# The first batch's k and v cast on their way in, half tables mirrored, and the residual summed in PSUM

## The chip, the cores and the metric

The kernel runs on one core of a Trainium2 chip. The metric is the device time of one execution in microseconds (us), here as a median of three runs. The engines are called as in the profile: PE (TensorE matmul), PEld (its weight load), DVE (VectorE), ACT (ScalarE), POOL (GpSimd), SP (SyncE). DMAs are issued from SP (the hardware queue) and from POOL (the software queue).

## The reference

The computation has two stages. The first is a retention recurrence per batch and head, the second mixes the result by a Fourier transform over positions and channels, adds it to itself, normalizes, and runs two dense layers with a residual. There are 4 batches, 8 heads, 768 positions, a head width of 64, so a model width of 512 and a hidden width of 2048.

```python
gamma = 1.0 - 2.0 ** (-5.0 - np.arange(H))
for t in range(S):
    state = gamma * state + einsum('bhd,bhe->bhde', k[:, :, t], v[:, :, t])
    y[:, :, t] = scale * einsum('bhd,bhde->bhe', q[:, :, t], state)
x = y.transpose(0, 2, 1, 3).reshape(B, S, H * D)

mixed = np.real(np.fft.fft(np.fft.fft(x, axis=1), axis=2))
u = x + mixed
un = (u - mean(u)) / sqrt(var(u) + 1e-6)
out = u + relu(un @ w_ch1) @ w_ch2
```

## The kernel before

**Recurrence.** Positions are cut into 6 chunks of 128, heads are taken two at a time (four head pairs, in the order 0, 1, 3, 2; index `i` counts in that order). Per pair, q and k are turned by PE transposes (`tq`), their products (`wkA`) are masked by DVE into `atm` (L471 in the first batch, L603 later), chunk states (`wkK`) are run forward by a scan (L495) or by steps (L629), and the two parts of y are summed in PSUM (`wkY`) and evicted to `x` by ACT (L539, L662).

**Mixing.** The transform uses symmetry. `fold_s` builds sums and differences of the two halves of the positions (`xab`, L679), `fold_d` of the channels (`eo`, L689); `s1_unit` (L736) multiplies by the position tables `csp`, `ssp` to give `g`; `s2_unit` (L849, L853) multiplies `g` by the channel tables `cd16`, `sd16` and DVE puts both halves of `u` together from P and Q (L862, L864) with `qn`, an eviction of Q by ACT (L861). `g0_unit` makes the column that the folds leave out. For the first three of the six blocks of 128 rows of batch 0, x itself is put into the same PSUM tile by `px_unit` (L803) with halved identities. The tables are made in the kernel: `trig_dve` makes reduced angles on DVE (L288 to L292), `t_act` takes sines on ACT (L316 to L325).

**Dense layers.** `h0_unit` (L953) for the first half of batch 0, by blocks of 128 rows and groups of four of the 16 hidden blocks; `h_unit` (L936) elsewhere; `ch_unit` (L979, four parts per 128 rows) is the second layer. The weights come in eight pieces: four `w1_unit` (L993) and four `w2_unit` (L1000), casting DMAs issued from POOL.

**Order.** SP issues batch 0's loads first: q, k, v of each pair, f32, 384 KB each (L165). `first_units()` is a list written out by hand. Each unit's instructions are pinned behind the earlier ones on each engine (`pin`), so that every engine works its part of the list in that order. `filler(n)` puts n matmuls without use on PE. What follows the list is emitted by `emit`: the streams of `majors` (the dense layers) and of the next batch's attention are spread over a common axis and sorted; the place of a major in batch 0 is its number divided by their count. The second batch's loads (`load_unit(1, i, 6)`) wait for the seventh of the eight weight pieces, `w_dma[6]`, and for `lb[0]["mm"]`, the last matmul of the eighth `h0_unit`:

```python
if after is not None:
    for x in (w_dma[after].ins, lb[0]["mm"].ins):
        tc.add_manual_dep(dma.ins, x.name, ...)
```

In batch 0 POOL casts q (L398), scales and casts k (L407, L410) and casts v (L423) from f32 tiles; in batch 1 `cast_unit` does the same (L373, L383, L388).

Of the kernel before, what the change touches and what calls it, by code (L numbers as in the profile page):

```python
# [18 lines left out]
P = 128  # L19
# [10 lines left out]
PAIR_ORDER = [0, 1, 3, 2]  # L30
ON_ACT = {'q': (0, 1, 0), 'kv': (1, 1, 1), 'g': (0, 1, 1), 'gr': (0, 0, 0)}
# [12 lines left out]
def kernel(  # L44
# [13 lines left out]
    def pool(name, bufs, **kw):  # L58
# [3 lines left out]
    inp = pool("inp", 11)  # L62
# [33 lines left out]
        "p (n w) -> p n w", n=4)  # L96
    pmask = const.tile([P, 4], f32, tag="pmask")
# [60 lines left out]
    def load_unit(b, i, after=None):  # L158
        def run():
            h0 = 2 * PAIR_ORDER[i]  # L160
            for name, src in srcs.items():
                t = inp.tile([P, 2, NCH, D], f32, tag="in32", name=f"{name}32")
# [17 lines left out]
    for i in range(4):  # L180
        load_unit(0, i)()
# [3 lines left out]
    icol = const.tile([P, 8], f32, tag="icol")  # L185
    lgrow = const.tile([P, H], f32, tag="lgrow")
    gexp = const.tile([P, 2, H], f32, tag="gexp")
    gq8, gkd = gexp[:, 0], gexp[:, 1]
# [3 lines left out]
    kf_i = tmp[:, 0, 0:KN].bitcast(i32)  # L192
    kf = tmp[:, 1, 0:KN]
    rs = [tmp[:, 2 + n] if n < 4 else tmp2[:, n - 4] for n in range(10)]
# [6 lines left out]
    nc.gpsimd.iota(kf_i, pattern=[[1, KN]], base=0, channel_multiplier=0)  # L201
    nc.gpsimd.memset(wz, 0.0)  # L202
    filler(6)()
    for h in range(H):
        nc.vector.memset(lgrow[:, h:h + 1], float(lng[h]))
    nc.vector.memset(maskf, 1.0)
    nc.vector.tensor_copy(icol[:, 0:6], icol_i[:, 0:6])
    nc.vector.tensor_scalar(out=gexp[:, 0], in0=lgrow, scalar1=icol[:, 3:4],
                            scalar2=float(math.log(0.125)), op0=ALU.mult, op1=ALU.add)
    nc.vector.tensor_scalar(out=gexp[:, 1], in0=lgrow, scalar1=icol[:, 5:6], scalar2=None,  # L210
                            op0=ALU.mult)
    nc.scalar.activation(gexp, gexp, AF.Exp, bias=0.0, scale=1.0)
    for h2 in range(2):
        nc.scalar.activation(gk2[D * h2:D * h2 + D], lgrow[D * h2:D * h2 + D, h2:H:2], AF.Exp,
                             bias=0.0, scale=float(P))
    nc.scalar.activation(icol[:, 6:7], lgrow[:, 0:1], AF.Sin, bias=0.0, scale=1.0)
    make_identity(nc, ident16)
    nc.gpsimd.affine_select(out=maskf, in_=maskf, compare_op=ALU.is_ge, fill=0.0, base=0,
                            pattern=[[1, P]], channel_multiplier=-1)
    nc.gpsimd.memset(hpi, float(np.pi / 2))  # L220
    nc.gpsimd.memset(epsT, 1e-6)
    nc.gpsimd.memset(gk5[:, :, :, 0:1], 0.0)
    nc.vector.tensor_scalar(out=icoln[:, 0:3], in0=icol[:, 0:3],
                            scalar1=float(np.float32(1.0 / S)), scalar2=None, op0=ALU.mult)
    nc.vector.tensor_scalar(out=icoln[:, 3:5], in0=icol[:, 3:5], scalar1=float(1.0 / DM),
                            scalar2=None, op0=ALU.mult)
    nc.vector.tensor_copy(kf, kf_i)

    def gk_unit(hp):
        def run():  # L230
            nc.scalar.copy(gk5[:, hp, :, 1:], gk2[:, hp:hp + 1].unsqueeze(1).to_broadcast(
                [P, D, NCH - 2]))
        return run
# [7 lines left out]
    def half_tables():  # L241
        nc.vector.tensor_scalar(out=last[:, 0:1], in0=icol[:, 0:1], scalar1=float(P - 1),
                                scalar2=1.0, op0=ALU.is_equal, op1=ALU.mult)
        for n, (m, a) in enumerate(((-0.5, 1.0), (-1.0, 1.0), (-2.0, 0.0))):
# [8 lines left out]
                                scalar2=1.0, op0=ALU.mult, op1=ALU.mult)  # L253
        nc.vector.tensor_scalar(out=t2[:, 3, 0:128], in0=sd16[:, 0, 1:257:2], scalar1=halve,
                                scalar2=1.0, op0=ALU.mult, op1=ALU.mult)
# [11 lines left out]
    m2 = const.tile([P, 1], f32, tag="m2c")  # L267
    odd = const.tile([P, 1], f32, tag="oddc")

    def parity_consts():  # L270
        nc.vector.tensor_scalar(out=m2, in0=icol[:, 0:1], scalar1=0.5, scalar2=-0.25,
                                op0=ALU.mult, op1=ALU.add)
        nc.vector.tensor_scalar(out=m2, in0=m2, scalar1=MAGIC, scalar2=-MAGIC,
                                op0=ALU.add, op1=ALU.add)
        nc.vector.scalar_tensor_tensor(out=odd, in0=m2, scalar=-2.0, in1=icol[:, 0:1],
                                       op0=ALU.mult, op1=ALU.add)
        nc.vector.tensor_copy(pmask[:, 1:4:2], odd.to_broadcast([P, 2]))
        nc.vector.tensor_scalar(out=pmask[:, 0:4:2], in0=pmask[:, 1:4:2], scalar1=-1.0,
                                scalar2=1.0, op0=ALU.mult, op1=ALU.add)
        nc.vector.tensor_scalar(out=sgn, in0=odd, scalar1=-2.0, scalar2=1.0,  # L280
                                op0=ALU.mult, op1=ALU.add)

    def trig_dve(idx, n, w, col, coln):
        r = rs[2 * idx][:, 0:w]
        ra = rs[2 * idx + 1][:, 0:w]

        def run():
            nc.vector.tensor_scalar(out=ra, in0=kf[:, 0:w], scalar1=coln, scalar2=MAGIC,  # L288
                                    op0=ALU.mult, op1=ALU.add)
            nc.vector.tensor_scalar(out=ra, in0=ra, scalar1=-MAGIC, scalar2=float(n),  # L290
                                    op0=ALU.add, op1=ALU.mult)
            nc.vector.scalar_tensor_tensor(out=r, in0=kf[:, 0:w], scalar=col, in1=ra,  # L292
                                           op0=ALU.mult, op1=ALU.subtract)
        return run

    def ts_dve(c):
        return trig_dve(c, S, KN, icol[:, c:c + 1], icoln[:, c:c + 1])

    def csn_unit(c):
        def run():  # L300
            nc.scalar.activation(csn[:, c, :], rs[2 * c + 1][:, 0:384], AF.Sin, bias=hpi,
                                 scale=-float(2.0 * np.pi / S))
        return run

    def td_dve(c):
        return trig_dve(3 + c, DM, 257, icol[:, 3 + c:4 + c], icoln[:, 3 + c:4 + c])

    def t_act(idx, part):
        w = KN if idx < 3 else 257
# [4 lines left out]
        def run():  # L314
            if part == 0:
                nc.scalar.activation(ra, r, AF.Abs, bias=0.0, scale=1.0)  # L316
            elif idx < 3:
                src = (ra, r)[part - 1].rearrange("p (i t) -> p t i", t=2)
                dst = (csp, ssp)[part - 1]
                nc.scalar.activation(dst[:, :, idx, :], src, AF.Sin,  # L320
                                     bias=hpi if part == 1 else 0.0,
                                     scale=-sc if part == 1 else sc)
            else:
                src, dst = (ra, r)[part - 1], (cd16, sd16)[part - 1]
                nc.scalar.activation(dst[:, idx - 3, :], src, AF.Sin,  # L325
                                     bias=hpi if part == 1 else 0.0, scale=-sc)
# [4 lines left out]
    for j in range(2):  # L331
# [7 lines left out]
        nc.gpsimd.memset(t[:, 0:257:256], 0.0)  # L339
        qns.append(t)  # L340

    hid, nhid = xts[1][:, 0, 0, 0:P], xts[1][:, 0, 1, 0:P]
# [7 lines left out]
    def half_ids():  # L350
        nc.gpsimd.tensor_scalar(out=hid, in0=ident16, scalar1=0.5, scalar2=1.0, op0=ALU.mult,
                                op1=ALU.mult)
        nc.gpsimd.tensor_scalar(out=nhid, in0=ident16, scalar1=-0.5, scalar2=1.0, op0=ALU.mult,
                                op1=ALU.mult)

    x_edges(0)()


    at, q16_of, kd_of, v16_of, last_cast = {}, {}, {}, {}, {}

    def cast_unit(b, i):
        def run():
            h0 = 2 * PAIR_ORDER[i]
            q32, k32, v32 = (in_of.pop((n, b, i)) for n in "qkv")
            kd = kp.tile([P, NCH, 2, D], f16, tag="kd16", name="kd16")
            v16 = vp.tile([P, NCH, 2, D], f16, tag="v16", name="v16")
            with ExitStack() as es:
# [14 lines left out]
                for h2 in range(2):  # L382
                    kc = nc.gpsimd.tensor_scalar(out=kd[:, :, h2, :], in0=k32[:, h2],  # L383
                                                 scalar1=gkd[:, h0 + h2:h0 + h2 + 1],
                                                 scalar2=1.0, op0=ALU.mult, op1=ALU.mult)
                    if b < NPE:
                        es.enter_context(tc.issue_after(kc.ins))
                last_cast[b, i] = nc.gpsimd.tensor_scalar(  # L388
                    out=v16, in0=v32.rearrange("p h c d -> p c h d"), scalar1=1.0, scalar2=1.0,
                    op0=ALU.mult, op1=ALU.mult)  # L390
            q16_of[b, i], kd_of[b, i], v16_of[b, i] = q16, kd, v16
# [10 lines left out]
    def k0_unit(i):  # L402
        def run():
            h0 = 2 * PAIR_ORDER[i]
            k32 = in_of.pop(("k", 0, i))
            kd = kd_of[0, i] = kp.tile([P, NCH, 2, D], f16, tag="kd16", name="kd16")
            nc.gpsimd.tensor_scalar(out=kd[:, :, 0, :], in0=k32[:, 0], scalar1=gkd[:, h0:h0 + 1],  # L407
                                    scalar2=1.0, op0=ALU.mult, op1=ALU.mult)
            if i < 3:
                nc.gpsimd.tensor_scalar(out=kd[:, :, 1, :], in0=k32[:, 1],  # L410
                                        scalar1=gkd[:, h0 + 1:h0 + 2], scalar2=1.0,
                                        op0=ALU.mult, op1=ALU.mult)
            else:
                nc.scalar.activation(kd[:, :, 1, :], k32[:, 1], AF.Copy, bias=0.0,
                                     scale=gkd[:, h0 + 1:h0 + 2])
        return run
# [765 lines left out]
```

## Time and profile before

| what | value |
|---|---|
| median of 3 runs | 246.93 us (246.65 to 247.16) |
| the profiled execution: span from first to last instruction | 245.4 us (its own time is given by this span; no other is listed) |
| median less span | 1.5 us |
| PE busy | 234.2 us (95%) |
| DVE, ACT, POOL busy | 177.0, 124.2, 81.7 us (72, 51, 33%) |
| fillers L151 | 40 matmuls, 13.5 us |
| first `h0` matmul, first `psc` matmul | 35.08 us, 48.44 us |
| granted TensorE clock | 1.000 |
| DMA, share of 16 engines' span: SP's queue, POOL's queue | 62.2%, 10.7% |

How to read it. In the page's rows of digits each digit is the busy share of one fortieth of the span, 6.1 us, in tenths. A timeline line has the start in us, the duration in us, the engine, the line of the kernel, the operation, output and inputs, shapes, the count, and in brackets the idle time before it with what ended it. A line of waits has the waiting engine and line, whom it waited for, the total in us, the number of times and the longest. A line of a window has the stretch, then busy us and instructions of PE, PEld, DVE, ACT and POOL, the granted clock, the DMA share and GB/s. Matmul durations overlap, so the spacing of starts is what one costs.

### The profile page before, as it was taken

The page shows a single profiled execution, that of the slowest core. Times are in us where ns is not written, and L with a number is a line of the kernel's source. Part 1 is how long each engine was busy: PE and PEld are TensorE (multiplying, and loading weights), DVE is VectorE, ACT ScalarE, POOL GpSimd, SP SyncE. Part 2 cuts the span into 40 slices and gives each one's busy share as a digit, 9 for nine tenths or more (in the row PEclk, how much of TensorE's full clock was granted, in tenths as well). Part 3 has the DMA queues.
Part 4 walks back from the last instruction along what each step waited for, and adds up shares of the span by engine and source line. Part 5 has one row for each costly group of instructions (what it writes and reads, how often), then busy time and mean ns, then how long its engine had stood idle before and what let it go on. Part 6 is the DMA issues. An engine that isn't in the chain of part 4 may idle for free.

```text
span 245.4 us, 5309 instructions
## 1 busy us (share of the span) xinstructions
PE 234.2 (95%) x2024; PEld 143.8 (59%) x2024; DVE 177.0 (72%) x430; ACT 124.2 (51%) x276; POOL 81.7 (33%) x146
## 2 busy tenths in 40 slices
PE   6997899999999998999999999999999999999995
PEld 2454668956776655665567546655666455445543
DVE  8997957897897788996885748887895656424112
ACT  8798669587775434751247414742247317202500
POOL 6667601465600057690000646660002405000000
PEclk9999999999999999999999999999999999999999
DMA  8999999699999377999999667786200241221012
GB/s 173 256 260 140 204 195 205 164 245 230 291 229 222 75 168 165 191 181 137 256 272 214 116 141 203 129 120 139 87 1 0 45 151 21 47 85 43 0 45 85
DMA packets 99209, 36.39 MB, mean 148 GB/s; under 512 B 89840, under 2 KB 96240, under 8 KB 99184
## 3 DMA queue, kind: packets, MB, share of 16 engines
q1 hardware_dynamic: 94960, 31.86, 62.2%
q0 software_dynamic: 4224, 4.19, 10.7%
q8 instruction: 16, 0.26, 0.5%
q14 instruction: 9, 0.07, 0.1%
HBM read 27.26 MB, written 6.29 MB: 137 GB/s over the span
## 4 chain that ended last, share of the span: by engine, by line
PE 71%; DMA 7%; DVE 7%; POOL 4%; ACT 4%; SPq 3%; issue 1%; POOLq 0%; ACTq 0%; DVEq 0%
PE psc L979 30%; PE psh L936 25%; DMA k<-in_k_dram 5%; PE ps L736 3%; SPq L165 3%; PE wkA L600 3%; DMA q<-in_q_dram 2%; PE wkY L654 2%; PE pq L833 2%; PE wkY L650 1%; POOL u L870 1%; PE wkK L619 1%; ACT un L885 1%; DVE bst L889 1%; POOL kd L407 1%
## 5 line engine op out<-in xcount | busy, mean ns | idle before, releaser
L979 PE MATMUL psc<-w,ht 128*128 128x512 f16 (+2 forms) x400 | 89.3, 371 | 0.0
L936 PE MATMUL psh<-unT,w 128*128 128x384 f16 x448 | 81.6, 326 | 0.4 <-ACT ht L940 0.2
L979 PEld LDWEIGHTS <-ht 128*128 128x128 f16 x400 | 37.5, 98 | 36.5 <-issue 0.2
L936 PEld LDWEIGHTS <-w 128*128 128x128 f16 x448 | 42.3, 98 | 24.7 <-issue 1.4
L940 ACT ACTIVATE ht<-psh 128x384 f16<-128x384 f32 x64 | 30.9, 489 | 41.7 <-PE psh L936 41.1
L870 POOL TENSOR_TENSOR u<-u,x 128x256 f32<-128x256 f32 x21 | 13.3, 635 | 100.3 <-DVE u L840 91.0
L983 DVE SCALAR_TENSOR_TENSOR ob<-psc,stats,u 128x512 f32<-128x512 f32 (+2 forms) x25 | 18.1, 726 | 26.1 <-PE psc L979 26.0
L942 DVE TENSOR_SCALAR ht<-psh 128x384 f16<-128x384 f32 x48 | 26.2, 548 | 7.7 <-PE psh L936 7.4
L603 DVE TENSOR_TENSOR atm<-wkA,maskp 128x512 f16<-128x512 f32 x36 | 23.8, 681 | 1.6 <-PE wkA L600 1.6
L891 ACT ACTIVATE un<-u,stats 128x512 f16<-128x512 f32 x21 | 15.2, 722 | 16.7 <-DVE stats L890 12.1
L889 DVE BATCH_NORM_STATS2 bst<-u 128x6 f32<-128x512 f32 x21 | 14.6, 694 | 7.7 <-POOL u L872 7.6
L629 DVE SCALAR_TENSOR_TENSOR s<-s,gk,wkK 128x128 f16<-128x128 f16 x48 | 16.3, 341 | 3.7 <-ACT s L625 2.7
L662 ACT ACTIVATE x<-wkY,gexp 128x384 f16<-128x384 f32 x24 | 12.8, 581 | 8.0 <-PE wkY L654 8.0
L151 PE MATMUL wps<-ht 128*128 128x512 f16 x40 | 13.5, 444 | 2.2 <-POOL ht L202 2.2
L383 POOL TENSOR_SCALAR kd<-k,gexp 128x384 f16<-128x384 f32 x24 | 13.8, 585 | 3.6 <-DMA k<-in_k_dram 3.6
L872 POOL TENSOR_TENSOR u<-u,x 128x256 f32<-128x256 f32 x21 | 13.3, 635 | 3.0 <-DVE stats L890 3.0
L600 PE MATMUL wkA<-qTz,kT 128*128 128x256 f16 x72 | 13.4, 273 | 0.1
L835 ACT COPY qn<-pq 128x128 f32<-128x128 f32 x18 | 4.9, 272 | 13.6 <-PE pq L833 13.6
L953 PE MATMUL psh<-unT,w 128*128 128x128 f16 x192 | 11.5, 219 | 0.1
L953 PEld LDWEIGHTS <-w 128*128 128x128 f16 x192 | 11.0, 98 | 0.7 <-issue 0.5
L840 DVE SCALAR_TENSOR_TENSOR u<-pq,g,qn 128x256 f32<-128x256 f32 x18 | 8.5, 472 | 3.3 <-PE psh L936 2.5
L388 POOL TENSOR_SCALAR v<-v 128x768 f16<-128x768 f32 x12 | 10.0, 831 | 1.3 <-DMA v<-in_v_dram 1.3
(164 smaller groups left out, 315.6 us busy)
## 6 DMA issues: line engine op xcount, KB each, us to landing
q<-in_q_dram SPq DMA_DIRECT2D x16, 384.0 KB, 6.3
k<-in_k_dram SPq DMA_DIRECT2D x16, 384.0 KB, 5.6
v<-in_v_dram SPq DMA_DIRECT2D x16, 384.0 KB, 6.3
out_dram<-ob SPq DMA_DIRECT2D x23, 256.0 KB, 2.6
w<-in_moe_w_ch_dram POOLq DMA_DIRECT2D x8, 512.0 KB, 10.8
unT<-un SPq DMA_TRANSPOSE x15, 2.4
out_dram<-ob SPq DMA_DIRECT2D x1, 192.0 KB, 1.9
qTz<-q16z SPq DMA_TRANSPOSE x8, 3.9
```

Of the source, the lines that this page charges most:

```text
L600: mm = nc.tensor.matmul(wk[:, c2], st["kT"][:, c, :], st["qT"][:, :, c, :], start=True, stop=True)
L603: nc.vector.tensor_tensor(out=st["atm"][:, 2 * part:2 * part + 2], in0=wk, in1=maskp[:, PAIR_ORDER[i]].unsqueeze(1).to_broadcast([P, 2, 2, ...
L629: nc.vector.scalar_tensor_tensor(out=s16[:, c], in0=s16[:, c - 1], scalar=gk2[:, hp:hp + 1], in1=wk[:, c - c0], op0=ALU.mult, op1=ALU.add)
L870: nc.gpsimd.tensor_tensor(out=u[:, kb, 0:256], in0=u[:, kb, 0:256], in1=x[:, kb, 0, 1:257], op=ALU.add)
L889: nc.vector.bn_stats(bst, u[:, kb, :])
L891: una = nc.scalar.activation(un, u[:, kb, :], AF.Identity, bias=stats[:, kb, 0:1], scale=-1.0)
L936: nc.tensor.matmul(psh, w116[:, cb, fb * P:(fb + 1) * P], unT[:, cb, rt * 384:(rt + 1) * 384], start=(cb == 0), stop=(cb == 3))
L940: nc.scalar.activation(ht16[:, fb, :], psh, AF.Relu, bias=0.0, scale=-1.0)
L942: nc.vector.tensor_scalar(out=ht16[:, fb, :], in0=psh, scalar1=-1.0, scalar2=0.0, op0=ALU.mult, op1=ALU.max)
L953: mm = nc.tensor.matmul(psh[:, f], w116[:, cb, fb * P:(fb + 1) * P], unT[:, cb, kb * P:(kb + 1) * P], start=(cb == 0), stop=(cb == 3))
L979: nc.tensor.matmul(psc[:, c0:c1], ht16[:, fb, rb3 * P:(rb3 + 1) * P], w216[:, fb, c0:c1], start=(fb == 0), stop=(fb == NFB - 1))
L983: nc.vector.scalar_tensor_tensor(out=ob[:, c0:c1], in0=psc[:, c0:c1], scalar=lb[b]["st"][:, rb, 3:4], in1=lb[b]["u"][:, rb, c0:c1], op0=AL ...
```

## The change

Nothing of the result changes, only how batch 0 is prepared and in which order, and how v of batch 1 comes in.

- k and v of batch 0 are loaded by one DMA per head pair issued from POOL that casts f32 to f16 on the way (`kl_unit`, `vl_unit`); SP loads only q, in the order 0, 1, 3, 2. v of batch 1 comes the same way, at the end of the list. The casts of v and the f32 k tiles go; k is scaled from f16 by POOL, DVE or ACT (`k0_unit`). k is transposed unscaled, 12 transposes per pair for 6, and the mask factor comes from `gkm`.
- The trig tables are computed for half their width and mirrored (`mir_s`, `mir_d`); `csn` is copied from `csp`. Steps are given to POOL, ACT or DVE by a letter.
- For the first three blocks of batch 0, x enters PSUM by `ident16`, the lower and upper half of the channels by their own matmuls, with turned tables `cdr`, `sdr` (`turn_d`) for the upper half; `s2e_unit` has 8 matmuls for 4, and un and u are taken straight from PSUM (`un0_unit`, `u0_unit`); `qn` and the two DVE steps are not used there.
- The second half of the first mixing step is cut into parts that start before the last pair is done (`s1a_pre`, `s1b_pre`, then `s1a_fin`, `s1b_fin`).
- The list `first_units()` is in a new order. It now holds the 12 `h0_unit`s, whose places among the majors are taken by 12 empty ones (two transposes' places go).

```diff
+LOADS = (('q', 0), ('q', 1), ('q', 3), ('q', 2))
+SW, DW = 194, 129
...
-    for i in range(4):
-        load_unit(0, i)()
+    for name, i in LOADS:
+        load0(name, i)
...
+    def trig(idx, part, eng):
...
+            if part == 0 and eng == "A":
+                nc.scalar.activation(ra, kf[:, 0:w], AF.Copy, bias=MAGIC, scale=icoln[:, c:c + 1])
...
+    def mir_s(which, eng):
...
+            scaled(eng, dst, src, (sgn, nsgn)[which])
...
+    def mir_d(which, eng):
...
+            scaled(eng, tab[:, :, DW:257], src, (nsgn, sgn)[which])
...
+    def turn_d(which, eng):
+        def run():
+            scaled(eng, (cdr, sdr)[which], (cd16, sd16)[which][:, :, 1:256], nsgn)
+        return run
...
+    def csn_unit(t, eng):
+        def run():
+            dst = csn.rearrange("p c (i t) -> p t c i", t=2)[:, t]
+            src = csp[:, t, :, 0:192]
...
+                if b > 1:
+                    v16 = v16_of[b, i] = vp.tile([P, 2, NCH, D], f16, tag="v16", name="v16")
...
+    def kl_unit(i):
         def run():
             h0 = 2 * PAIR_ORDER[i]
...
+            k16_of[i] = kin.tile([P, 2, NCH, D], f16, tag="k16", name="k16")
+            nc.gpsimd.dma_start(k16_of[i], k[0, h0:h0 + 2].rearrange("h (c p) d -> p h c d", p=P))
...
+    def vl_unit(b, i):
+        def run():
+            h0 = 2 * PAIR_ORDER[i]
+            v16_of[b, i] = vp.tile([P, 2, NCH, D], f16, tag="v16", name="v16")
+            nc.gpsimd.dma_start(v16_of[b, i],
+                                v[b, h0:h0 + 2].rearrange("h (c p) d -> p h c d", p=P))
...
+    def k0_unit(i, h2, eng="V"):
...
+                (nc.vector if eng == "V" else nc.gpsimd).tensor_scalar(
+                    out=dst, in0=src, scalar1=gkd[:, h:h + 1], scalar2=1.0, op0=ALU.mult,
+                    op1=ALU.mult)
...
+    def s1a_fin(par):
+        def run():
+            for e in range(2):
+                s1_last(1, e, 0, 64, False, (par,))
...
+            for n, (dst, rhs) in enumerate(((lo[:, 0:256], x[:, 0, 1:257]),
+                                            (lo[:, 256:257], x[:, 1, 257:258]),
+                                            (up, x[:, 1, 256:1:-1]))):
+                nc.tensor.matmul(dst, ident16, rhs, start=n == 0 or n == 2 and kb in SPLIT,
+                                 stop=False, skip_group_check=True)
...
+    def s2e_unit(kb, cb, halves=(0, 1)):
+        def run():
+            g = fd[0]["g"]
+            for half in halves:
+                for e in range(2):
+                    tab = ((cd16, sd16), (cdr, sdr))[half][e]
+                    nc.tensor.matmul(lb[0]["pq", kb, half], g[:, 2 * e + cb, kb * P:kb * P + P],
+                                     tab[:, cb], start=False, stop=cb == 1 and e == 1,
+                                     skip_group_check=True)
...
+    def un0_unit(kb, half, eng):
...
+            if eng == "A":
+                una = nc.scalar.activation(un, pq, AF.Identity, bias=xm, scale=-1.0)
...
+            lb[0]["n"] = lb[0].get("n", 0) + 1
+            if lb[0]["n"] == 8:
                 lb[0]["mm"] = mm
...
-            for kb in range(3):
-                if kb:
-                    majors.append(unT_unit(0, kb))
-                majors += [h0_unit(kb, g) for g in range(4)]
+            majors += [lambda: None] * 12
```

The part of the new list that POOL works, in its order (P marks a step given to POOL by letter): k loads 0 and 1 with a memset between them and one trig step behind; q cast 0; identity; a trig step; q cast 1; mask; v loads 0 and 1; k load 2; q cast 3; edge memsets; k load 3; v load 2; q cast 2; v load 3; `w1_unit(0)`; `k0_unit(2, 0)`, `k0_unit(2, 1)`; `mir_s(1)`; `k0_unit(3, 0)`; `w1_unit(1)`; `mir_s(0)`; the two `fold_s` of 774 elements and one of 390; `turn_d(0)`; `csn_unit(0)`; `w1_unit(2)`, `w1_unit(3)`, `w2_unit(0)`; `gr_unit(2)`; edges of the other x; `w2_unit(1)`; `gr_unit(3)`; `w2_unit(2)`, `w2_unit(3)`; then the four v loads of batch 1. The end of the list, for all engines:

```python
x0_unit(3, 1, "A"), s1b_pre(1), x0_unit(3, 0, "A"), xmean_unit(0), fold_d(0, 0, (0,), "V"),
fold_d(0, 0, (1,), "V"), mir_d(0, "A"), s1_mm(0), turn_d(0, "P"), s1_mm(1),
fold_s(0, 130, 258, 1, 2, (1,), "V"), s1a_fin(1), csn_unit(0, "P"),
fold_s(0, 130, 258, 1, 2, (0,), "V"), s1a_fin(0), s1b_fin(1), g_unit(1, "V"), ga_unit("V"),
w1_unit(2), g_unit(0, "A"), s1b_fin(0), px_unit(0), s2e_unit(0, 0, (0,)), csn_unit(1, "A"),
gb_unit(1, "V"), s2e_unit(0, 1, (0,)), un0_unit(0, 0, "A"), s2e_unit(0, 0, (1,)), ...
un0_unit(0, 1, "A"), unT0(0, 1), ... ut0(0, 1, "V"), ut0(0, 0, "A"), h0_unit(0, 0),
un0_unit(1, 2, "V"), px_unit(2), unT0(1, 2), s2e_unit(2, 0, (0,)), ... h0_unit(0, 1), ...
```

553 lines of the change are left out of this document (312 added, 241 removed).

## The prediction

> **What bounds the kernel now.** I read the page first, then PE's waits from 35 us on, then windows of 2 us around the seams, then the timelines of PE and POOL. From the page:
>
> ```profile
> span 245.4 us, 5309 instructions
> ...
> PE   6997899999999998999999999999999999999995
> ...
> DMA  8999999699999377999999667786200241221012
> ```
>
> PE is full from the sixth slice (35 us) on; before that it runs fillers (L151) and waits. DMA is full for the first seven slices, then again for the second batch. Who makes PE wait after 35 us:
>
> ```profile
> PE pst L920 <- ACT un L891: 0.7, 1, 0.7
> PE tq L556 <- POOL kd L383: 0.3, 1, 0.3
> PE ps L779 <- DVE xg L770: 0.2, 1, 0.2
> PE psh L936 <- ACT ht L940: 0.2, 1, 0.2
> PE psh L936 <- DVE ht L942: 0.2, 1, 0.2
> ```
>
> That is 1.6 us in 210. So nothing gained behind 35 us counts; what counts is when PE's full stretch begins, and whether it stays full. Its beginning, and the first place where it nearly breaks (PE's timeline):
>
> ```profile
> 35.08 3.00 PE L953 MATMUL psh<-unT,w 128*128 128x128 f16 x48
> ...
> 48.44 1.03 PE L979 MATMUL psc<-w,ht 128*128 128x512 f16 x4
> ...
> 56.90 0.51 PE L556 MATMUL tq<-ident,kd 128*128 128x128 f16 x6 [0.30 <-POOL kd L383]
> ```
>
> Two marks follow from it: `h0` starts at 35.08, the first `psc` at 48.44. At 56.90 the second batch's k transposes already wait for data. The seams of the DMA, last two columns (share, GB/s written):
>
> ```profile
> 18.00:20.00 2.00, 1.57 (x25) 0.74 (x23) 1.54 (x4) 1.97 (x5) 0.36 (x1) 1.00 1.34 227
> 20.00:22.00 2.00, 1.48 (x21) 1.03 (x21) 2.00 (x5) 1.85 (x5) 1.96 (x3) 1.00 0.49 82
> 42.00:44.00 2.00, 2.00 (x40) 2.00 (x38) 1.98 (x5) 1.07 (x4) 1.23 (x2) 1.00 1.09 180
> 44.00:46.00 2.00, 2.00 (x38) 1.98 (x36) 1.83 (x5) 1.33 (x3) 0.00 (x0) 1.00 0.16 26
> ```
>
> Batch 0's loads end near 20.7, the weights run from 22.2 to 44.0, so 21.8 / 8 = 2.72 us each; the second batch's loads start at 44.89 and come from 46.3 on. POOL's timeline gives the prices:
>
> ```profile
> 20.41 0.96 POOL L993 DMA_DIRECT2D w<-in_moe_w_ch_dram  x1
> 21.41 1.27 POOL L407 TENSOR_SCALAR kd<-k,gexp 128x384 f16<-128x384 f32 x1
> ...
> 25.38 2.99 POOL L1000 DMA_DIRECT2D w<-in_moe_w_ch_dram  x4
> ...
> 55.69 1.15 POOL L383 TENSOR_SCALAR kd<-k,gexp 128x384 f16<-128x384 f32 x2 [0.89 <-DMA k<-in_k_dram]
> ```
>
> A casting DMA costs POOL 2.99 / 4 = 0.75 to 0.96 us, for 512 runs of 2 KB. The k and v loads have 1536 runs of 256 B.
>
> **Part 1: POOL until the folds.** From POOL's list go 8 casts and scalings of k and v; 8 casting issues come in, of price d. The rest, in the new order, by rows: constants and memsets 3.6; four q casts at 0.83, 3.3; two trig steps 0.7; three k scalings at 0.585, 1.75; two mirrors of 576 elements, between the rows of 384 (0.585) and 768 (0.83), 1.4; two w1 issues 1.55; three sums of x on POOL. POOL's only two-input row is `u`, 0.635 for 256 elements; in proportion, less a fixed part, 774 elements cost 1.8 (between 0.83, the one-input row of 768, and 1.92) and 390 cost 0.95: 4.55. Together 16.9 + 8d.
>
> One data wait lies in it. Today the POOL casts meet k at 6.07, v at 7.70, q at 8.85, k at 10.68, so v takes 1.65, q 1.15, k 1.83 of DMA time, and the first data count from 3.1. Moved by either ring I keep these: the runs read are the same (below that only if half the written bytes count). Ahead of the third k are four q, three k, two v: 3.1 + 4.6 + 5.5 + 3.3 = 16.5. POOL's first k scaling, which waits for it, is reached at 8.4 + 8d, 14.7 for d = 0.78, so issues are free up to d = 1.01. Queued behind that wait are the mirrors, w1(1) and the three folds, 8.5 us, and DVE waits for these: the folds end at 25.0.
>
> d itself no row shows. Bounds: 0.75 (nothing per run) and 3 × 0.78 = 2.35 (all of it per run). I take at most 1.0: seven issues of 512 runs differ by under 0.05, the 0.96 is the first one, and 512 runs in 0.75 us leave little time for each.
>
> **Part 2: DVE, ACT and the loads.** DVE from the first mask (9.9, as today): 16 masks at 0.465 spacing (1.94 / 4), 7.4; four scans 2.9; one kT copy 0.8; a fold 0.3: 21.4 without waits. The last v lands at 3.1 + 18.5 = 21.6 as today; then products 0.5, scan 0.8, masks and fold 1.3, products and two x evictions 1.0: 25.1. ACT up to the last x: exponents and table loads to 4.1 as today, five copies of 768 at 0.70, eight x at 0.53, three k scalings 1.8, gk 1.4, the sign turns 1.8, 17 trig steps of about 0.35 (half of today's widths, between the 0.20 of one element and the 0.53 of 386): 22.8, not the last. So POOL, loads and DVE end together near 25, against 28.3 for x and 30.4 for the last fold today.
>
> **Part 3: from the folds to h0.** Two eo sums 1.0, two half sums 0.6, the last short matmuls 0.3, two g copies 1.0 (one beside them), `s2e` 0.5, two centring steps on ACT 1.0, a row sum 0.65, half a transpose copy 0.4, hand-overs 0.3: 5.5 us, `h0` at 30.5. Gone are qn, the two u steps and the mean from g0. Today the same stretch takes 35.08 − 28.26 = 6.8 from x. The extra matmuls (48 short ones for 12; eight `s2e` for four per block, 0.45 us more; 12 transposes of k for 6) stand before `h0` in PE time that fillers hold now; for block 2 they stand inside. Inside `h0`'s stretch today: 13.36. After: 192 × 0.0565 = 10.85, block 2 with its px and transposes 1.65, blocks 3 to 5 1.35: 13.85. First `psc` at 44.35, 4.1 earlier.
>
> **Part 4: the second batch's loads.** They wait for w2's third piece and the eighth `h0` group (39.5). Pieces w1(2) and later stand behind `turn_d` and `csn` on POOL, and `turn_d` waits for ACT's mirror, 26.2: issue at 27.6, data from 28.9, while w1(1) is through at 26. Six pieces × 2.72: the third w2 at 42.5, the last at 45.2. The second batch's q thus starts at 43.2, near today's 44.89, although PE wants it 4.1 earlier. And the four v (6.6 us) now queue behind w2 in POOL's ring and share the engines with q and k. Served by halves, k of pairs 0 and 1 lands at 50.5 and 56.2; today 50.28 and 55.69. One psc group more (0.87) stands ahead, since the empty majors leave 54 where there were 56. Then pair 1's transposes come at 56.2 + 1.15 = 57.35 against 56.90 and only 0.87 − 0.45 = 0.4 of the 4.1 stays. Served first, q and k land by 50.5 for pair 1 and all 4.1 stay. The removed v casts (0.83 each) only shorten POOL's queue behind k, which hides them. Between 0.4 and 4.1 I take the middle, 2.2: neither how the rings share nor what a casting run costs has a row here. The sum is in the span: 245.4 − 2.2 = 243.2. The page names no other time for this execution; the median lies 1.5 above the span and I leave that: 246.9 − 2.2 = 244.7.
>
> The Trainium skill, "DMA: Bandwidth & Descriptors", Queues, rings and completion order, states that each engine takes the queues in turn, a packet at a time, which if packets were alike would mean halves, so 246.5. No run here shows two rings at work together.
>
> **Rivals.** (a) *The second batch keeps the whole gain*: a casting run under 1.2 us per load, or q and k served first. For: half the bytes written. Against: k's 256 B runs take 1.83 where q's long runs take 1.15, so runs, not bytes, set the time. 242.8.
>
> (b) *The software ring is served first*, from three quarters of the service on slower than before: all v ahead of k. v ends at 45.2 + 6.6 = 51.8, pair 0's k at 54.7, its transposes at 55.9 against 53.76 today: 2.1 late, less 0.87, so 1.3 slower, 248.2. For: v is issued by 38, q at 43. Against: q's long runs hold an engine longer per turn than v's, and no row of today shows two rings together.
>
> (c) *POOL becomes the bound*: each us of d above 1.01 costs 8 us at the folds. At d = 1.52 the 4.1 are gone; at 2.35 it is 6.6 slower, 253.5. For: kd at 21.41 took 1.27 instead of 0.585 while DVE folded x, and DVE's L290 took 0.86 instead of 0.36 beside POOL; eight issues that each lost those 0.69 would come to 1.44 to 1.65. Against: seven w issues ran beside a busy DVE at 0.75 to 0.80. The Trainium skill, "SBUF — State Buffer", Who interferes with whom, says that a DVE operation using both port pairs shuts GpSimd out, descriptor writing included, which speaks for (c); the rows of w do not show it, the row of kd shows a wait of that kind.
>
> (d) *It does not do what it says*: k and v are still read from HBM as f32; a DMA that is as full as before would leave 0 ± 0.5.
>
> **How the numbers follow.** The forecast case (0.4 to 3.7 gained) 0.50, (a) 0.18, (b) 0.14, (c) 0.11, (d) 0.07. About 0.2%, 0.5 us, is what a measurement of this kernel can tell from no change (runs from 246.65 to 247.16). Faster: 0.50 + 0.18 = 0.68. Same: 0.07. Slower: 0.25. Low end 242.4, just past (a); high end 248.4, just past (b); beyond it lies the dear half of (c), and below it a little of (a).
>
> **What would show it.** Casting issues of k and v on POOL at or under 1.0; above 1.5 is (c). `h0` near 30.5 and the first `psc` near 44.4. The `tq` transposes of k in the second batch waiting for POOL's kd, 2 us in all: nothing there is (a), 5 us is (b). A gap in the DMA row near 26 to 29. PE behind 65 us as full as before; if it is not, my belief that only the front moves is wrong.

## The result, and the profile after

The changed kernel takes 250.54 us (249.84 to 251.66, 4 runs), the kernel before 246.88 (246.65 to 247.16, 4 runs): 1.0148 times as long, 95% interval 1.012 to 1.0175. It is 3.66 us slower where 2.2 us faster was forecast, and outside the range. Each trace below is of one execution; those of e4, e10 and e16 lie 1.9, 0.9 and 1.2 us above the medians of their kernels.

The page of after follows. Its lines stand against the first three shown of before; the row of the granted clock (PEclk) is added, which is full throughout in before.

```profile
span 248.7 us, 5403 instructions
...
PE   7897999996999997999999999999999999999994
...
PEclk9999599999999999999999999999999999999999
DMA  7999099999769314997989068997200241221012
```

Three things are new. DMA has a hole in the fifth slice (25 to 31 us), the clock is at half in the same slice, and PE has a dent in the tenth (56 to 62 us), where before was full. Who makes PE wait from 35 us on:

```profile
PE tq L618 <- POOL kd L435: 2.3, 2, 1.1
PE pst L1113 <- ACT un L1087: 1.0, 1, 1.0
PE wkY L712 <- ACT kT L629: 0.4, 2, 0.2
PE wkK L681 <- POOL v L443: 0.4, 1, 0.4
PE ps L922 <- DVE xg L913: 0.2, 1, 0.2
```

The wait of `tq` for `kd` grew from 0.3 to 2.3 us, and all but the last of these lines are new or longer than in before (two lines of 0.2 us, as in before, are left out). PE's timeline at the marks of the prediction:

```profile
33.44 1.05 PE L1143 MATMUL psh<-unT,w 128*128 128x128 f16 x16
...
47.04 4.48 PE L1170 MATMUL psc<-w,ht 128*128 128x512 f16 x20
51.36 0.39 PE L1113 MATMUL pst<-ident,un 128*128 128x128 f16 x4
51.58 2.97 PE L1170 MATMUL psc<-w,ht 128*128 128x512 f16 x13
...
54.76 1.89 PE L1170 MATMUL psc<-w,ht 128*128 128x512 f16 x8
...
58.49 0.51 PE L618 MATMUL tq<-ident,kd 128*128 128x128 f16 x6 [1.12 <-POOL kd L435]
```

`h0` starts at 33.44 (before 35.08), the first `psc` at 47.04 (before 48.44): 1.4 us were gained there, and lost again behind it. The same stretch in before, from its first `psc` to its first `tq`:

```profile
48.44 1.03 PE L979 MATMUL psc<-w,ht 128*128 128x512 f16 x4
...
49.53 1.03 PE L979 MATMUL psc<-w,ht 128*128 128x512 f16 x4
...
50.62 1.89 PE L979 MATMUL psc<-w,ht 128*128 128x512 f16 x8
...
52.56 1.03 PE L979 MATMUL psc<-w,ht 128*128 128x512 f16 x4
53.43 0.50 PE L556 MATMUL tq<-ident,q16z 128*128 128x128 f16 x6
```

The counts at the line ends matter: 20 + 13 + 8 `psc` stand ahead of the first `tq`, where before had 4 + 4 + 8 + 4. The windows of the hole (last three columns: granted clock, DMA share, GB/s):

```profile
24.00:26.00 2.00, 1.44 (x29) 1.16 (x24) 2.00 (x4) 0.80 (x2) 0.35 (x1) 0.50 0.13 21
26.00:28.00 2.00, 2.00 (x22) 1.94 (x20) 1.19 (x4) 1.59 (x5) 0.00 (x0) 0.50 0.00 0
48.00:50.00 2.00, 2.00 (x11) 0.89 (x10) 1.40 (x5) 0.37 (x1) 0.95 (x2) 1.00 2.31 158
```

In the last row only POOL's queue moves packets, the last weights and then v: share 2.31, but 158 GB/s. Before has 240 to 263 in windows of 8 us from 48 to 72 us, at a share of 1.2. How the two queues of after share the engines shows in the packets by queue (packets, MB, share of 16 engines), first from 46.8 to 51 us, then from 54 to 56:

```profile
q0 software_dynamic: 3676, 0.70, 200.5%
...
q1 hardware_dynamic: 827, 0.21, 80.0%
q0 software_dynamic: 827, 0.11, 79.9%
```

SP issues q at 46.77, but up to 51 us none of its queue's packets (q1) moves; from 54 to 56 both queues move the same number. POOL's timeline:

```profile
9.48 1.03 POOL L461 DMA_DIRECT2D k<-in_k_dram  x1
...
20.21 4.14 POOL L741 TENSOR_TENSOR xab<-x 128x774 f16<-128x774 f16 x3
28.34 0.70 POOL L354 TENSOR_SCALAR gk<-cd,nsgn 128x510 f16<-128x510 f16 x1 [3.99 <-ACT cd L352]
...
29.75 1.58 POOL L1184 DMA_DIRECT2D w<-in_moe_w_ch_dram  x2
...
57.29 1.15 POOL L435 TENSOR_SCALAR kd<-k,gexp 128x384 f16<-128x384 f32 x2 [2.20 <-DMA k<-in_k_dram]
```

Casting issues cost about 1.03; the sums end at 24.35; then POOL stands for 3.99 us at `turn_d` with six weight loads queued behind it; and the second batch's first k is there at 57.29, in before at 50.28.

Three marks per kernel, from PE's and DVE's timelines (start of the first `psc`; of the second batch's first `ps`, the first row sums L736 or L873; end of the last `ob`), split the difference to before. After and e1 have 63 `psc` between the first two marks, the others 56; seven at 0.216 us are 1.51 us of work only moved forward, and are taken off there and added behind.

| us against before | to first psc | on to first ps | on to last ob | in all |
|---|---|---|---|---|
| before (marks 48.44, 82.17, 242.86) | 0 | 0 | 0 | 0 |
| after (47.04, 85.54, 245.97) | −1.40 | +3.26 | +1.25 | +3.11 |
| e1, weights early (46.60, 83.78, 244.20) | −1.84 | +1.94 | +1.24 | +1.34 |
| e9, and h0 in the stream (46.70, 82.73, 243.50) | −1.74 | +2.30 | +0.08 | +0.64 |
| e11, and front filled (45.52, 81.90, 242.80) | −2.92 | +2.65 | +0.21 | −0.06 |
| e13, as e11 but v from SP (46.21, 81.19, 243.03) | −2.23 | +1.25 | +1.15 | +0.17 |
| e16, e11 and all sums on DVE (46.69, 81.67, 242.62) | −1.75 | +1.25 | +0.26 | −0.24 |

The first column also holds the clock of the execution traced: e1, e9 and e16 have half clock for 3.4 us (from 24.3, 11.8 and 11.3 us), after for 6.8 us (from 23.8), e11 and e13 not at all.

So the loss has parts behind the first `psc`, and the experiments name most of them.

### The profile page after: what moved, and what is told of

It reads as the page before. It is cut to its first block, busy times and chain, and to the rows that moved or that the text cites. A ratio compares the mean times of both kernels' runs of the same rounds, so it can differ in the third digit from the quotient of the medians.

```text
span 248.7 us, 5403 instructions
## 1 busy us (share of the span) xinstructions
PE 236.4 (95%) x2082; PEld 147.6 (59%) x2082; DVE 175.7 (71%) x420; ACT 120.9 (49%) x272; POOL 91.1 (37%) x152
## 4 chain that ended last, share of the span: by engine, by line
PE 69%; DVE 11%; POOL 8%; DMA 4%; ACT 3%; issue 3%; SPq 1%; POOLq 0%; ACTq 0%
PE psc L1170 26%; PE psh L1126 23%; DMA k<-in_k_dram 4%; PE psh L1143 4%; DVE atm L533 3%; PE wkA L662 3%; PE ps L873 2%; PE wkY L716 2%; PE wkY L712 2%; SPq L172 1%; POOL u L1074 1%; POOL u L1072 1%; DVE xab L741 1%; DVE bst L1085 1%; DVE u L1051 1%
## 5 line engine op out<-in xcount | busy, mean ns | idle before, releaser
L1170 PE MATMUL psc<-w,ht 128*128 128x512 f16 (+2 forms) x400 | 88.1, 370 | 0.0
L1126 PE MATMUL psh<-unT,w 128*128 128x384 f16 x448 | 83.1, 326 | 0.4 <-ACT ht L1130 0.2
L1126 PEld LDWEIGHTS <-w 128*128 128x128 f16 x448 | 42.1, 98 | 23.8 <-issue 1.5
L1174 DVE SCALAR_TENSOR_TENSOR ob<-psc,stats,u 128x512 f32<-128x512 f32 (+2 forms) x25 | 18.0, 725 | 27.0 <-PE psc L1170 26.5
L665 DVE TENSOR_TENSOR atm<-wkA,maskp 128x512 f16<-128x512 f32 x36 | 23.9, 684 | 2.5 <-PE wkA L662 2.5
L156 PE MATMUL wps<-ht 128*128 128x512 f16 x29 | 10.0, 491 | 1.3 <-DVE ht L217 1.3
L662 PEld LDWEIGHTS <-kT 128*128 128x128 f16 x72 | 6.8, 98 | 5.7 <-DMA kT<-kd 0.6
```

The source lines that it names most:

```text
L662: mm = nc.tensor.matmul(wk[:, c2], st["kT"][:, c, :], st["qT"][:, :, c, :], start=True, stop=True)
L665: nc.vector.tensor_tensor(out=st["atm"][:, 2 * part:2 * part + 2], in0=wk, in1=maskp[:, PAIR_ORDER[i]].unsqueeze(1).to_broadcast([P, 2, 2, ...
L1126: nc.tensor.matmul(psh, w116[:, cb, fb * P:(fb + 1) * P], unT[:, cb, rt * 384:(rt + 1) * 384], start=(cb == 0), stop=(cb == 3))
L1170: nc.tensor.matmul(psc[:, c0:c1], ht16[:, fb, rb3 * P:(rb3 + 1) * P], w216[:, fb, c0:c1], start=(fb == 0), stop=(fb == NFB - 1))
L1174: nc.vector.scalar_tensor_tensor(out=ob[:, c0:c1], in0=psc[:, c0:c1], scalar=lb[b]["st"][:, rb, 3:4], in1=lb[b]["u"][:, rb, c0:c1], op0=AL ...
```

## Experiments

**e1: the weight loads ahead of turn_d.** Theory then: the late weights and the shared queues bring k late.

```diff
- turn_d(0, "P"), ... w1_unit(2), ... w1_unit(3), ... w2_unit(0), ... w2_unit(3),
+ w1_unit(2), w1_unit(3), w2_unit(0), w2_unit(1), w2_unit(2), w2_unit(3), turn_d(0, "P"),
```

> The changed kernel with its last six weight issues put ahead of turn_d in the list, where POOL sat idle for 3.99 us. Late loads (the DMA stands empty from 24.3 to 31 because the weight issues queue behind turn_d, so the second batch's q and k start at 46.8): the empty stretch shrinks to under 2 us, the loads start near 42, PE's waits for kd go from 2.3 to under 0.5 us, the median falls by 2.5 to 4 to 246.5 to 248. Shared rings (v of the second batch on POOL's ring takes the engines from q and k): v is still ahead, PE still waits 1.5 us or more, 249 to 250. Clock (PE at half speed from 22.6 to 30.6): no change but a run-to-run one, 250.0 to 251.

248.67 us (before, run beside it, 246.98; ratio 1.0069, 1.0043 to 1.0096). The second batch's q is issued at 41.90 instead of 46.77, and no wait of `tq` for `kd` is left. 2.0 of the 3.66 us came back, and 1.7 stayed although PE no longer waited for k.

**e2: the second batch's v in float32 from SP again**, cast on GpSimd as before the change.

```diff
- if b == 1 and name == "v": continue
- vl_unit(1, 0), ... vl_unit(1, 3),
```

> The changed kernel with v of the second batch loaded as f32 from SP and cast by POOL as before; nine f32 tiles for eight. Shared rings: the k loads of the first two pairs land 3 to 5 us earlier than in the changed kernel, the median falls by 1.5 to 3 to 247.5 to 249. Late loads: q still starts near 46.8, later than before's 44.9, so k lands 2 us later than before and most of the loss stays, 249 to 250.5. Clock: 250 to 251.

248.37 us (1.0053, 1.0037 to 1.0068). q is issued at 47.39, later than in after, and still PE never waits for `kd`. Without the casting loads beside it, k lands 5.2 us after its issue (47.80); in after it takes 10.0 (47.18), in before 4.8 (45.35). Most of the difference is the wait for the first packet: SP's queue moves it 1.0 us after q's issue in before and e2, 4.3 us after it in after. So of the 7.0 us that k lands later in after than in before, 5.2 are this longer way and 1.8 the later issue. Each of the two edits takes over 4 us off (k lands at 52.8 in e1, 53.0 in e2, 57.2 in after), and either alone is enough to end the wait.

**e3: e1 and e2 together.**

> Both edits. If late loads and shared rings together make the whole loss, the front's gain of 1.4 us is kept: 245 to 246. If the clock or something else makes it, 249 or more.

248.98 us (1.0072, 1.0052 to 1.0092): nothing adds up. What is left of the loss has to do with neither.

**e4: before, with only the second batch's v by casting loads**, issued at the end of the first batch's list.

```diff
+ un += [vl_unit(1, i) for i in range(4)]
```

> The kernel before with one part of the change alone: v of the second batch by four casting DMAs, issued from POOL at the end of the first list (v lies as head, chunk in its tile, as in the changed kernel). Shared rings: v queues behind the weights and shares the engines with q and k from 45 on, k lands 3 to 6 us later, 1 to 3 us slower, 248 to 250. Late loads alone: the loads start as before and v is only cast elsewhere, 246.5 to 247.2.

248.68 us (1.0082, 1.0051 to 1.0113), with all else as before except the order of v within its tile. The trace is of the slowest of five executions, 250.57 us. PE's timeline and windows there:

```profile
55.55 0.79 PE L567 MATMUL tq<-ident,kd 128*128 128x128 f16 x6 [1.95 <-POOL kd L384]
56.13 3.33 PE L990 MATMUL psc<-w,ht 128*128 128x512 f16 x8
```

```profile
54.00:55.00 1.00, 0.00 (x0) 0.00 (x0) 1.00 (x7) 0.98 (x2) 0.74 (x2) 1.00 1.17 239
56.00:58.00 2.00, 2.00 (x9) 0.87 (x7) 0.00 (x0) 0.80 (x1) 1.42 (x3) 0.50 1.08 247
```

The casting loads alone cost 1.7 us by the median, which is about what the wait for k grew by, from 0.30 to 1.95. In the execution traced, half clock followed, and eight `psc` took 3.33 us instead of 1.89. The other four executions have a mean clock of 0.998 to 1.000 against 0.993 here, so the median holds no such stretch.

**e5 to e8: the order.** New theory: the list now holds all twelve `h0` units, and everything that the streams emit stands behind its end, first of all `s2` of row blocks 3 to 5 (L1060, L1063). In before these ran between the `h0` units at 38 to 46 us; after, at 45.7. The `psc` that would cover the second batch's chain are spent ahead of it. The first try put these units into the list:

```diff
- h0_unit(2, 3), ... h0_unit(2, 2), ... h0_unit(2, 0),
+ h0_unit(2, 3), s2_unit(0, 3), ... h0_unit(2, 2), s2_unit(0, 4), ... h0_unit(2, 0), s2_unit(0, 5),
```

e6 adds e1's edit, e7 only its first two units, e8 six fillers to e7 (`filler(4)` ahead of `s1b_pre(0)`, `filler(2)` ahead of `yi_unit(3, 1)`).

> After, with the three s2 units of row blocks 3, 4 and 5 of the first batch (the matmuls pq L1060 and L1063, the two evictions, the residual additions and norm) put between the last h0 units of the list instead of behind all of them; 28 instead of 41 psc matmuls then stand on PE's stream ahead of the second batch's first tq. Theory ORDER (the list holds all twelve h0 units, so everything that the streams emit, these s2 units first, comes behind the whole h0 stretch; pst then starts 7 us later, the psc matmuls that cover the second batch's chain are used up ahead of it, and the chain runs bare on PE): first pst L1113 within 1 us of the first psc instead of 4.3 us behind it, ACT un wait of 1.0 us gone; but k still lands late here, so the wait of tq for kd grows by what tq comes earlier: 249 to 250.5. Rival LOADS (all of the loss is k and v sharing the DMA engines and the late weights): 250.5, unchanged.

> After, with the six weight loads ahead of turn_d as in the run e1 (no wait of tq for kd was left there, 248.67) and the three s2 units between the h0 units as well. Theory ORDER: the second batch's attention is covered again, the 2 us of short waits of PE between the first psc and the first ps of the second batch, and about 1 us of them behind that, go: 245.5 to 247. Rival LOADS: those waits have nothing to do with where s2 stands: 248.7 as e1. Rival CLOCK (the rest of e1's loss is TensorE at half clock at 24 to 28 us): 248.7 as well, since the clock drops here too.

> As e6, but only the first two of the six weight units (w1 2 and 3) ahead of turn_d, which then has GpSimd free when ACT has mirrored the table (27.7 us); the four others stay where the change has them. Theory ORDER: as e6 within 0.7 us if the second batch's q and k still start by 44 us; if they start at 46 us as in after, tq waits for kd by some 1 to 2 us: 246 to 248.5. Rival LOADS: 248.7 to 250.5.

> As e7, with six more filler matmuls of 512 columns on PE at 22 to 25 us, where it waits for GpSimd's sums (four ahead of s1b_pre(0), two ahead of yi_unit(3, 1)). Theory CLOCK (the granted clock falls to half because PE was idle for more than half of 22 to 24 us; at full clock the 6 us of matmuls from 25 to 31 us take some 2.5 us less): clock 1.00 in 24 to 30 us, h0 starts near 31 instead of 33.4 us, and 1.5 to 2.5 us less than e7. If the fillers only push back what stands behind them, or DVE's and ACT's chain sets h0's start (e1 and e3, which had full clock from 28 us on, began h0 at 33.0 and 33.4 all the same): as e7 within 0.5 us.

252.86 (1.0229, 1.0205 to 1.0253), 252.03 (1.02, 1.018 to 1.022), 252.21 (1.0203, 1.0178 to 1.0227) and 251.61 (1.0179, 1.0143 to 1.0215): all slower than before, and none is where its expectation had it. PE's timeline of e6 shows why:

```profile
50.22 0.40 PE L1113 MATMUL pst<-ident,un 128*128 128x128 f16 x4 [2.42 <-ACT un L1087]
51.27 6.16 PE L1170 MATMUL psc<-w,ht 128*128 128x512 f16 x20 [0.66 <-ACT ht L1151]
```

Units of the list are pinned in its order on every engine, the centring at the end of `s2` too; ACT and DVE stood at it, and `h0`'s evictions behind them. So these runs moved the stall and could not judge the theory. e7 against e8 did answer one thing, the clock: 0.50 at 26 to 28 us in e7 and 1.00 in e8, `h0` at 32.72 and 31.13.

**e9 and e12: the order, unpinned.** The last eight `h0` units go from the list back to the stream of large units, so that `s2` is emitted among them as before and nothing pins ACT and DVE. e9 has e1's edit too, e12 does not.

```diff
- majors += [lambda: None] * 12
+ majors += [lambda: None] * 4 + [h0_unit(...), ...]   # the list's last eight, same order
```

> After, with the six weight loads ahead of turn_d (as e1, 248.67, where tq never waited for kd), and with the last eight of the twelve h0 units taken out of the first batch's list and given back to the stream of large units, in the change's own order; the s2 units of row blocks 3 to 5 then stand among them as they did before the change, and nothing pins ACT and DVE to them (in e5 to e8 they were pinned in the list, and pst waited 3.1 us for un). PE then has 24 instead of 41 psc ahead of the second batch's first tq. Theory ORDER: e1's remaining loss goes, 245 to 247. Rival CLOCK (the front at half clock, not the order, is the rest of the loss): 248.7 as e1. Rival LOADS: 248.7.

> After, with only the eight h0 units given back to the stream; weights, turn_d and fillers as the change has them. Theory ORDER with LOADS as a separate part: the second batch's first tq comes earlier in PE's order, but its k lands no earlier than in after (57 to 66 us), so the waits of tq for kd grow: 249.5 to 251.5, no gain or a small one. If ORDER stands alone as the cause: 247 to 248.

e9: 247.67 us (1.0018, 1.0004 to 1.0033), 1.0 below e1. Its timeline has the seam of before again:

```profile
46.70 1.89 PE L1170 MATMUL psc<-w,ht 128*128 128x512 f16 x8
48.43 0.39 PE L1113 MATMUL pst<-ident,un 128*128 128x128 f16 x4
48.66 2.12 PE L1170 MATMUL psc<-w,ht 128*128 128x512 f16 x8
```

In the table, the 1.24 us behind the first `ps` are 0.08. e12: 253.00 (1.0247, 1.0216 to 1.0277), worse than after and than the 249.5 to 251.5 expected, as its waits tell: `tq` comes earlier while k does not, 3.50 us for `kd` and 1.89 for `q16z`. Order and late loads belong together: each hides part of the other.

**e10, e11, e15: the clock.** e15 is after with the six fillers alone; e10 is e1 with them and with `turn_d(0, "A")` behind `g_unit(0, "A")`; e11 is e10 and e9.

> After, with the six weight loads ahead, turn_d(0) on ACT behind g_unit(0) (so that GpSimd's queue of loads doesn't hold the lower half's table back), and six more filler matmuls on PE at 22 to 25 us; the h0 units stay in the list. Theory CLOCK: the clock stays at 1.00 through 24 to 31 us, h0 starts at 31 to 31.5 (33.0 in e1), and the end comes by as much earlier, 247 from 248.67. Theory ORDER: h0 starts earlier as well, but the second batch's chain still runs bare on PE between the first psc and the first ps of the second batch, so the loss behind h0 stays at some 3.4 us against before: 247 to 247.5, no better than before.

> e9 and e10 together: weights early, turn_d(0) on ACT, six fillers, eight h0 units in the stream. ORDER and CLOCK both: h0 starts at 31 to 31.5 us, first psc about 45, no bare chain behind it: 243 to 245.5, below before by 1.5 to 4. If either theory is wrong, the better of e9 and e10 within 0.5 us.

> After, with only the six fillers on PE at 22 to 25 us. CLOCK: granted clock 1.00 through 24 to 31 us and h0 about 1.6 us earlier (e8 against e7: 31.1 against 32.7); but k of the second batch comes no earlier, so tq waits for kd that much longer and the end gains little: 249.5 to 250.5. If the wait for kd does not take it: 248.5 to 249.

e15 has the clock at 1.00 there, `h0` at 31.24 and the first `psc` at 44.85, both within 0.8 us of the forecast:

```profile
24.00:26.00 2.00, 2.00 (x45) 1.63 (x42) 1.83 (x4) 1.26 (x3) 0.62 (x1) 1.00 0.08 13
```

and its PE timeline behind the first `psc`:

```profile
49.02 1.89 PE L1170 MATMUL psc<-w,ht 128*128 128x512 f16 x8 [1.42 <-DMA w<-in_moe_w_ch_dram]
...
58.05 0.51 PE L618 MATMUL tq<-ident,kd 128*128 128x128 f16 x6 [1.60 <-POOL kd L435]
```

And it takes 250.88 us (1.0156, 1.0123 to 1.0189), no less than after: of the 2.2 us gained at the first `psc` 1.7 are gone by the first `ps`, waited away for the last weights (1.42) and for k. So the half clock costs the change nothing that can be measured at its end as it stands. e10: 248.03 (1.0035, 1.0013 to 1.0057), with `h0` at 32.35, less early than the 31 to 31.5 expected. e11: 247.56 (1.0017, 0.9999 to 1.0035), not the 243 to 245.5 of both theories together. It is 2.92 us ahead at the first `psc` and loses 2.65 of it by the first `ps`, with 1.4 in one wait for `kd`: its first k was issued at 42.65 and was there at 52.93, while the four v, issued from 30.9 on, held the engines as well (share 1.57 to 2.44 from 42 to 50 us).

**e13, e14: where v stands.** e13 is e11 with e2's edit; e14 keeps v's casting loads and issues each behind its own pair's casts.

> e11 (weights early, turn_d(0) on ACT, fillers, eight h0 units in the stream: 247.56), with the second batch's v loaded from SP as float32 and cast by GpSimd, as before the change. In e11 the first k of the second batch was issued at 42.65 us and landed only at 52.9, while the four casting loads of v took the DMA engines at 44 to 48 us (156 to 165 GB/s), and tq waited 1.4 us for kd. Theory LOADS (the casting loads of v, issued at 31 us and waiting behind the weights, run ahead of q and k and bring k late): that wait goes, and the 2.9 us that e11 has gained at the first psc come through: 244.5 to 246.5. Rival FIXED (the second batch's loads are bound by what the DMA engines move in all; v in float32 moves twice as much, so k only changes place with v): 247 to 248.5.

> e11, with the four casting loads of v kept, but each issued behind the casts of its own pair's q and k on GpSimd instead of all four ahead. LOADS: k lands within 6 us of its issue, no wait of tq for kd above 0.5 us; v lands some 5 us behind kd, and wkK may wait for it: 244.5 to 247. FIXED: 247 to 248.5.

247.44 (1.0016, 0.9999 to 1.0033) and 248.37 (1.0051, 1.0028 to 1.0073); e14's one trace is of an execution of 484.24 us and says nothing of the others. In e13 the wait for `kd` is gone and the first `ps` is at 81.19, 1.0 earlier than before; at 108.8 a wait of 1.0 us of `wkK` for ACT's x, in the third batch's attention, takes that back. The wait went as expected, but the end did not follow.

**e16, e17: the three sums on DVE**, in e11 and e13.

```diff
- fold_s(0, 0, 258, 0, 1, (0,), "P"), ... (1,), "P"), ... fold_s(0, 0, 130, 1, 2, (0,), "P"),
+ fold_s(0, 0, 258, 0, 1, (0,), "V"), ... (1,), "V"), ... fold_s(0, 0, 130, 1, 2, (0,), "V"),
```

> e11 (weights early, turn_d(0) on ACT, fillers, eight h0 units in the stream: 247.56), with the three sums of x that the change put on GpSimd (4.35 us at 20.3 to 24.6 in e11) on DVE, whose sums of 774 and 780 elements take 0.55 us in before. Theory PORT (a two-input sum on DVE takes 1.2 to 2.0 us beside GpSimd's and 0.36 alone, so GpSimd's part costs DVE about what it spares): all four sums are done by 23.5 us instead of 24.6, and the weight loads follow at once: issued from 20.5 instead of 24.6 us, so the second batch's q and k start 3 us earlier, at 39 instead of 42.2, and tq waits less for kd: 245 to 246.5. If DVE becomes the front's bound instead (h0 later than 31.9 us): 247 to 248.

> e13 (as e11, the second batch's v as float32 from SP: 247.44), with the same three sums on DVE. PORT: as e16, weights and loads 3 us earlier; e13 had no wait of tq for kd left, so the gain is only what h0 gains, 0 to 1 us: 246.3 to 247.4; less than e16 if the casting loads are then no longer in the way, as they would be through before q and k start.

```profile
22.09 1.12 DVE L741 TENSOR_TENSOR xab<-x 128x774 f16<-128x774 f16 x1
...
24.19 0.55 DVE L741 TENSOR_TENSOR xab<-x 128x774 f16<-128x774 f16 x1
```

e16: 246.15 us (before, run beside it, 247.03; 0.9984, 0.9961 to 1.0007); e17: 247.05 (1.0003, 0.9985 to 1.0021). GpSimd's three sums took 4.14 in after; DVE's two of 774 elements take 1.12 and 0.55 here. All four sums are done at 26.5, not by the 23.5 expected. The six weight loads are issued at 20.4 to 25.0 instead of 29.75 to 34.6, the DMA hole is closed (share 1.19 to 1.21 from 24 to 32), and no wait for `kd` is left although v still comes by casting loads. The expected earlier start of q did not come (42.54): q also waits for the eighth `h0` group. e16 is the only version with a median below before, and its interval takes in no change. Here the clock does count: the seven executions of e16 with a mean clock of 0.997 or more take 245.60 to 246.23 us, the five at 0.990 to 0.993, the traced one among them, 247.16 to 248.29. That the first seven lie below before is a split made afterwards, not an experiment.

## Why the prediction was wrong, point by point

**Part 1 held.** d was 1.03 (1.0 assumed, 1.01 the bound) and the sums took 4.14 against 4.55; they end at 24.35 against 25.0. Rival (c) in its form, d above 1.5, did not come. Its mechanism did, in another place: DVE's own sum beside GpSimd's took 1.97 where two of the like take 0.63 in before, which put the masks behind it 1.6 us back. The Trainium skill, "SBUF — State Buffer", Who interferes with whom, has two-input operations of DVE contend with a GpSimd instruction that reads; the trace agrees (1.97 beside GpSimd's sums).

**Parts 2 and 3 were too short at half clock.** The last x was forecast for 25.1 and ended at 27.08, with those 1.6 us in it; from there to `h0` it was 6.36 us instead of 5.5. The working took PE's durations at full clock. But PE stood 1.10 us for the sums at 22.4 and 0.56 for the masks at 24.6, and the clock was at half from 23.8 to 30.6. (The terms listed for 5.5 us add up to 5.75, or 5.25 if one g copy runs beside the other.) e15 has the two terms without it: last x at 26.26, then 4.98 to `h0` at 31.24, against 30.5.

**Part 4 failed, in three of its terms.** *Weights at 27.6*: they went out at 29.75, since `turn_d` began at 28.34, not 26.2; and q at 46.77 instead of 43.2. *Served by halves*: only in the end. From q's issue to k's landing the forecast has 7.3 us by halves (43.2 to 50.5) and 11.5 by rival (b), the software ring first (to 54.7). Measured are 10.4 in after (46.77 to 57.20) and 10.6 in e11 (42.24 to 52.84). For the first 4 us POOL's queue runs alone, as in rival (b); then the packets go one for one (827 and 827). The same first wait, 4.0 to 4.3 us, is in every trace in which v's casting loads were queued on POOL ahead of q's issue, except e16, where nearly half of them is through (2.1). Why SP's first packet waits stays open. The price in e4, 1.7 us, is near (b)'s 1.3. The Trainium skill, "DMA: Bandwidth & Descriptors", Queues, rings and completion order, has each engine alternate by packets; the trace agrees from 54 to 56 us, and not from 46.8 to 51. *One `psc` group more, 0.87*: it was 41 instead of 20 `psc` ahead of the first `tq`, about five groups of four. The step looked at the count of empty majors (54 for 56). What moves the order is that the list is pinned and everything of the streams stands behind it, so the emptied slots hold nothing and `s2` of blocks 3 to 5 cannot start within `h0`. This is the term that none of the rivals had.

**"PE behind 65 us as full as before"** was named as the belief to test, and it fell: from 82 to 102 us PE is busy 19.33 us in before and 18.34 in after. Early weights leave it at that (e1, 18.33), and the order gives it back (e9, 19.27).

**The sum.** Of the 4.1 at the first `psc` 1.4 were there; behind it 4.5 were lost: 1.3 (table) to 2.0 (medians) for late loads and some 1.2 for the order behind the first `ps` (e1, e9 in the table), the rest between the first `psc` and the first `ps`, where order and loads can't be told apart, as e12 shows. What stays open is a part of the 2.3 to 2.7 us that e9 and e11 lose there. The wait for `kd` is 1.2 to 1.4 of it. e13 and e16, where that wait is gone, still lose 1.25, of which the waits listed name 0.7 (`pst` for `un` 0.5, `wkA` for DVE's s 0.2).

## What to carry to other kernels

A stage that is made earlier is worth only what the next stage's data and its cover allow: e15 had 3.6 of the 4.1 us forecast for the front, and no gain at the end. When work moves from a freely placed stream into a pinned list, ask what else was placed among it, since that moves too. And when a wait is added to the engine that issues DMAs, count the loads behind it: one small table step held back six of them by 4 us.

## What the runs showed of the hardware

Half clock comes in stretches of 3.4 us or twice that. In after it was 1.00 to 23.5 us and 0.50 from 24.0 to 30.5, though PE was busy all of the time from 26 on. In e4 a gap of 1.95 us was followed by 0.50 from 56 to 59 us, with PE busy throughout. In e6 the clock fell at 24.4 and at 51.7 us, and each time it was back 3.4 us later. These two falls lie 27.3 us apart and those of e5 (24.5 and 48.4) 23.9, eight and seven times 3.41: as if the clock were set on a fixed raster, which is argued from these traces and not tested. The Trainium skill, "TensorE: Matmul & The Clock Gate", Part 1, names an idle window of about 3.4 us as what leads to half clock. The length agrees with these stretches, but ahead of the fall in after, at 23.8, the longest gap was 1.10 us (22.4 to 23.5), and with six fillers, which cut that gap to 0.52 us, the trace shows no fall there (e15).

The length of a gap alone does not decide it. e15 has gaps of 1.42 and 1.60 us behind 47 us and stays at 1.00, and one of after's four executions has a mean clock of 1.000, the others 0.986 to 0.993. What does decide it is not shown here.

A casting load costs GpSimd 1.02 to 1.06 us with 1536 runs of 256 B (the very first 1.23) and 0.75 to 0.79 with 512 of 2 KB: the price rises much less than the runs. And casting halves the bytes written, but not the time of a load: batch 0's wrote 155 GB/s at a share of 2.26 from 8 to 14 us, where the float32 loads of before wrote 252 at 1.28. By these rates 192 KB take some 1.3 us and 384 KB some 1.6, an estimate.
